# Two S4 convolution layers and SwiGLU layers on one core: a PSUM tile for each row tile of a down product, and the second chunk's exponents through TensorE

## The chip, the cores and the metric

One Trainium2 chip, one of its cores. The metric is the device time of one execution in microseconds; the time given for a kernel is the median of its runs. Engine names are those of the profile: PE is TensorE's matrix unit, PEld its weight loads, DVE is VectorE, ACT is ScalarE, POOL is GpSimd, SP is SyncE, whose queue issues most DMA transfers.

## What is computed

The input is one sequence of 2048 rows of 512 channels. It goes twice through a pair of layers, each added to its input after a layer norm:

```
K = real(sum_n C * exp(dt*A*l) * dt*B)          # [512, 2048], one kernel for both layers
y = causal convolution of layernorm(x) with K, over the 2048 rows, per channel
x = x + y + layernorm(x) * Dskip
h = layernorm(x);  x = x + (silu(h @ w_gate) * (h @ w_up)) @ w_down      # 512 -> 1376 -> 512
```

A has 128 complex states per channel. The convolution weights K are the same in both layers, so they are formed once.

## The kernel before, in words

**First stage, to about 300 us: the convolution weights.** The 512 channels are worked in 8 chunks of 64 (`ch`, lines 352 to 604). For a chunk, `re` and `im` hold the powers exp(dt*A*32a) for a = 0 to 64 with the 128 states on the partitions. They are made in parts:

- `gen_turns` and `gen_reduce` (DVE line 365, ACT lines 376 and 382, DVE lines 385 and 388) form the angles and take off whole turns; `gen_trig` (ACT lines 395 to 397) makes sines and cosines of them.
- The magnitudes exp(32a*rho) go to `re` (a = 1 to 32) and `mu` (a = 33 to 63). For chunks 2 to 7, `gen_mags` lets PE form the exponents 32a*rho as a matrix product into PSUM (line 438) and ACT takes one Exp over 1024 elements for each of four parts (line 441). The product's left side, `lts`, is rho split into three bf16 parts by POOL (`parts`, lines 423 to 426) and transposed by two DMAs (`turned`, line 430); its right side is a constant table (`tab`), loaded at line 989. For chunks 0 and 1, `gen_exp` makes them on ACT alone: 39 Exp of 64 elements (line 412) and four Square (line 415).
- `gen_e` (DVE lines 450 to 459) multiplies the magnitudes in; `gen_g` (DVE lines 467 to 499, with two accumulating DMAs from POOL's queue, lines 495 and 500) forms the coefficients `g`.
- `lags` (PE lines 510 and 511) multiplies both into `pk` in PSUM, ACT copies it to `ks` (line 516), `spread` (PE line 526) lays it out, ACT copies it to `kt`, and `spectra` (PE line 547) transforms it; ACT and DVE write the spectra out (lines 556 and 584 to 588).

Beside this, PE transforms the first two blocks of 512 normed rows by `direct` (line 286; the list `fw` for block 0, `early` and `second` for block 1). Block 0's rows are scaled by `norm_early` (DVE line 278). `gen_w` (DVE lines 183 to 187) forms the products dt*B*C for `g`. In this stage the order on PE, DVE and ACT is the order of the code, in which generators are advanced by hand (`take(g, 1)`); POOL and SP are ordered by a scheduler.

**Second stage.** The rows are worked in blocks of 512; `SEQ` gives the order of (layer, block). `ssm` of the next block (transform of its rows, DVE products with the spectra, lines 762 and 765, inverse transform on PE, line 781) is interleaved with `ffn` of the present one. `ffn` works two halves of 256 rows. For a half it makes six gate and up products `pgu` (PE lines 886 to 888; the remainder columns at lines 853 to 855), each evacuated by ACT (Silu, line 891; copy, line 893) and DVE (lines 892 and 894) into the fp16 pair `hh` and `hl`. Then comes the down product `py` (PE lines 900 to 902): 33 matmuls for each of its two row tiles of 128 rows. DVE scales each and adds it to `xt` (line 905), and a DMA stores the rows. In this stage a scheduler orders all engines; it tracks waits by tile.

`pgu`, `py`, and in the first stage `pm`, `pk` and `kp` come from one PSUM pool, `big`, of two slots, each of two banks:

```
    def pbig(shape, name):
        return ps.tile(shape, F32, name=name, tag="big", bufs=2)
```

Of the kernel before, what the change touches and what calls it, by code (L numbers as in the profile page):

```python
# [13 lines left out]
BF16 = mybir.dt.bfloat16  # L14
I32 = mybir.dt.int32
AF = mybir.ActivationFunctionType
OP = mybir.AluOpType
# [5 lines left out]
P = 128  # L23
# [58 lines left out]
def kernel(ctx, tc, x, a_re, a_im, b_re, b_im, c_re, c_im, log_dt, d_skip,  # L82
# [317 lines left out]
    def gen_exp(ch, ts):  # L400

        re, im, mu, xz, mz, t16 = ts
        r_ = rho[:, ch * DC:(ch + 1) * DC]
        for lv, m in enumerate(ZP):
            A.activation(mz[:, lv], r_, AF.Exp, scale=float(m))
            yield
        G.memset(re[:, :, 0], 1.0)
        if ch > 1:
            return
        for a0, o in ((0, re), (32, mu)):  # L410
            for a in [a for a in range(a0 + 1, a0 + 33) if a < 64 and (a % 2 or a % 8 == 0)]:
                A.activation(o[:, :, a - a0], r_, AF.Exp, scale=32.0 * a)
                yield
            for st in (2, 4):
                A.activation(o[:, :, st:33:2 * st] if a0 == 0 else o[:, :, st::2 * st],
                             re[:, :, (a0 + st) // 2:(a0 + 34) // 2:st], AF.Square)
                yield
# [11 lines left out]
        for c in range(2):  # L429
            nc.sync.dma_start_transpose(lts[:, c], pt[:, c].rearrange("p g q d -> p (g q d)"))  # L430

    def gen_mags(ch, ts):

        for k, o in enumerate((ts[0][:, :, 1:33], ts[2][:, :, 1:])):
            for h in range(2):
                pm = pbig([P, 32, 32], "pm")
                for e in range(2):
                    PE.matmul(pm[:, 16 * e:16 * e + 16], lhsT=lts[:112, ch % 2, h], rhs=tab[:112, k, e],
                              start=True, stop=True)
                yield  # L440
                A.activation(o[:, 32 * h:32 * h + 32], pm[:, :, :32 - k], AF.Exp)
                yield
# [426 lines left out]
    def ffn(layer, b, ready=None):  # L869
        for s in range(T // TB):  # L870
            rows = TB // P
            xt = xs[SEQ.index((layer, b)) % 3][:, s * rows:(s + 1) * rows]
            nh, nlo = ready if ready and s == 0 else ffn_norm(layer, b, s)
            hh = tl([P, FT, TB], "hh", "hh", F16)
            hl = tl([P, FT, TB], "hl", "hl", F16)
            for f0 in (0, 2, 4, 6, FT - 1, 8) if ready and s == 0 else (FT - 1, 0, 2, 4, 6, 8):
                pgu = pbig([P, 2, 2, TB], "pgu")
                if f0 == FT - 1:
                    remainder(pgu, nh, nlo, hh, hl)
                    continue  # L880
                for i in range(2):
                    fs = slice((f0 + i) * P, (f0 + i + 1) * P)
                    for wi in range(2):
                        o = pgu[:, wi, i]
                        for k in range(4):
                            PE.matmul(o, lhsT=wgu(wi, k, 0)[:, fs], rhs=nh[:, k], start=k == 0, stop=False)  # L886
                            PE.matmul(o, lhsT=wgu(wi, k, 0)[:, fs], rhs=nlo[:, k], start=False, stop=False)  # L887
                            PE.matmul(o, lhsT=wgu(wi, k, 1)[:, fs], rhs=nh[:, k], start=False, stop=k == 3)  # L888
                with tc.high_priority(offset=BOOST):
                    sg = tl([P, 2, TB], "sg", "sg")  # L890
                    A.activation(sg, pgu[:, 0], AF.Silu, scale=sc6[:, 3:4])  # L891
                    V.scalar_tensor_tensor(sg, pgu[:, 1], sc6[:, 4:5], sg, OP.mult, OP.mult)  # L892
                    A.activation(hh[:, f0:f0 + 2], sg, AF.Copy)  # L893
                    V.tensor_tensor(hl[:, f0:f0 + 2], sg, hh[:, f0:f0 + 2], OP.subtract)  # L894
            py = pbig([P, rows, D], "py")
            for r in range(rows):
                rc = slice(r * P, (r + 1) * P)
                for f in range(FT):
                    n = min(P, F - f * P)
                    PE.matmul(py[:, r], lhsT=hh[:n, f, rc], rhs=wd(f, 0)[:n], start=f == 0, stop=False)  # L900
                    PE.matmul(py[:, r], lhsT=hh[:n, f, rc], rhs=wd(f, 1)[:n], start=False, stop=False)  # L901
                    PE.matmul(py[:, r], lhsT=hl[:n, f, rc], rhs=wd(f, 0)[:n], start=False, stop=f == FT - 1)  # L902
                c = s * rows + r
                with tc.high_priority(offset=BOOST):
                    V.scalar_tensor_tensor(xt[:, r], py[:, r], sc6[:, 5:6], xt[:, r], OP.mult, OP.add)  # L905
                    if layer == NL - 1:
                        nc.sync.dma_start(out[0, b * T + c * P:b * T + (c + 1) * P, :], xt[:, r])
                    else:
                        nc.sync.dma_start(xdr[b, c], xt[:, r])
# [15 lines left out]
    with tc.manual_schedule(engines={mybir.EngineType.Activation, mybir.EngineType.DVE, mybir.EngineType.PE}):  # L925
# [10 lines left out]
        tr = gen_trig(ts[0])  # L936
        take(tr, 5)
        take(ex, 11)
        gen_w()
        norm_early(xe, ne, stats_x)  # L940
        fw = [direct(0, h, q, [ne[:, c, h * HD:(h + 1) * HD] for c in range(4)]) for h in range(2) for q in QORD]
        for f in fw:
            next(f)
# [8 lines left out]
        take(fw[1], 1)  # L952
        stats_x = stats(x1, 4, 1.0)
        take(fw[2], 1)
        for g in (gg, ge, gg, ge, gg, ge, gg, ge, gg, rd, gg, rd, gg, rd, gg, rd, gg, rd, rd, rd):
            take(g, 1)
        tr = gen_trig(ts[1])
        take(tr, 1)
# [12 lines left out]
        for g in (gg, ge, ge, gg, ge, ge):  # L971
            take(g, 1)
        ex = gen_exp(1, ts[1])
        take(ex, 14)
        take(fw[6], 1)
        take(ex, 13)
        take(fw[7], 1)
        mags = None
        take(early[0], 1)
        sp = iter(())  # L980
        for i in range(NCH - 1):
# [22 lines left out]
            norm_units(3, 9)  # L1004
            norm_units(0, 0)
            ks = spread_in(pk)
            if i == 0:
                take(early[1], 1)
            if mags:
                take(mags, 1)  # L1010
            if i % 2 == 0 and 0 < i < NCH - 2:
# [4 lines left out]
            if more:  # L1016
                rd = gen_reduce(ts[i + 2])
                next(rd)
            for g in (None, gg, None, gg, ge, gg, ge, gg, None, gg, None, rd, rd, ge, rd, rd, ge, rd, rd, rd, rd):
                take(g, 1) if g else wrap()  # L1020
            while tops:
# [19 lines left out]
            if more:  # L1041
                sp = spectra(i, kt, 0, NB, late=True)
                take(sp, 1)
                ex = gen_exp(i + 2, ts[i + 2])
                take(ex, 100)
                mags = gen_mags(i + 2, ts[i + 2])
                take(mags, 2)
                norm_units(3, 9)
                take(sp, 2)
                take(mags, 2)  # L1050
                take(sp, 2)
                norm_units(0, 0)
                sizes(i, kt, ks)
                take(ge, 2)
                wrap()
                take(ge, 1)
                wrap()
                take(ge, 1)
                take(gg, 1)
                while tops:  # L1060
                    tops.pop(0)()
                ts[i] = gs[i] = None
            else:
                sizes(i, kt, ks)
                take(ge, 4)
                take(gg, 1)
# [116 lines left out]
```

## Time and profile before

| | |
|---|---|
| runs shown | 1187.15, 1191.75 and 2940.31 us, median 1191.75 |
| the profiled execution | 1189.7 us, of which the traced span 1187.9 us |
| PE busy | 1108.9 us, 93% of the span |
| DVE busy | 1017.2 us, 86% |
| ACT busy | 621.3 us, 52% |
| POOL busy | 112.9 us, 10% |

A busy share is an average over stages. Matmuls overlap in the records, so the pace of PE is read from the distance between the starts of two matmuls, not from the length of one. An idle time in a list of waits stands with what ended it: "PE py L900 <- DVE xg L905" is time in which PE stood before a matmul of line 900 until the DVE instruction of line 905 was done. In a timeline the idle time before an instruction stands at the row's end, in brackets. "xne", "xg", "xf" and "mix" are the program's names for buffers that hold rows and their parts at that time.

### The profile page before, as it was taken

To read this page: it belongs to the slowest core of one execution; us is meant where nothing else is said; L and a number is where in the kernel's file an instruction comes from. 1 tells how busy PE (TensorE), PEld (TensorE's weight loads), DVE (VectorE), ACT (ScalarE), POOL (GpSimd) and SP (SyncE) were. 2 spreads that over 40 slices of the span, in tenths; PEclk is the share of its full clock that TensorE was granted. 3 is DMA by queue.
4 is the path that set the end of the run, shared out by engine and by line. 5 is a ranking of instruction groups with operands and counts; after the bars stand their busy time and mean duration, and the time that the engine had idled before them with its cause. 6 is when DMAs were issued, how large, how long until landed. Compare 5 with 4: busy or idle time off the path is not lost.

```text
span 1187.9 us, 25243 instructions
## 1 busy us (share of the span) xinstructions
PE 1108.9 (93%) x10268; PEld 862.1 (73%) x10268; DVE 1017.2 (86%) x1669; ACT 621.3 (52%) x1190; POOL 112.9 (10%) x166
## 2 busy tenths in 40 slices
PE   2999899889789989899999999999999999999998
PEld 2867677677675848687768687858687686877875
DVE  8979999998899998999999999989992899983211
ACT  6999889862383553538553534735432452334211
POOL 3100200004200010001000100111000010000000
PEclk9989999999899989999999999989999999999999
DMA  6445455577695238332343444324534144312000
GB/s 235 124 139 127 119 124 124 128 191 197 193 282 170 76 115 200 114 103 83 103 151 122 121 167 144 105 77 155 153 105 135 45 121 134 120 41 46 14 23 18
DMA packets 138455, 146.90 MB, mean 124 GB/s; under 512 B 77858, under 2 KB 87074, under 8 KB 138339
## 3 DMA queue, kind: packets, MB, share of 16 engines
q1 hardware_dynamic: 133474, 128.51, 36.0%
q0 software_dynamic: 4864, 16.78, 6.1%
q8 instruction: 80, 1.31, 0.5%
q14 instruction: 37, 0.30, 0.1%
HBM read 98.19 MB, written 28.31 MB: 106 GB/s over the span
## 4 chain that ended last, share of the span: by engine, by line
PE 37%; DVE 24%; issue 4%; ACT 3%; DMA 3%; SPq 1%; POOL 1%; DVEq 0%; ACTq 0%; POOLq 0%
PE pgu L886 5%; PE pgu L887 5%; PE pgu L888 5%; PE py L900 5%; PE py L901 5%; PE py L902 4%; DVE t L762 4%; PE pi L781 3%; DVE yk L765 3%; PE pf L270 3%; DVE z L226 2%; DVE yk L762 2%; DMA mix<-nn 2%; DVE sg L892 2%; DVE hl L894 2%
## 5 line engine op out<-in xcount | busy, mean ns | idle before, releaser
L886 PE MATMUL pgu<-mix,wsl 128*128 128x256 f16 x1280 | 351.1, 274 | 4.6 <-DVE mix L832 2.4
L887 PE MATMUL pgu<-mix,wsl 128*128 128x256 f16 x1280 | 351.1, 274 | 0.0
L888 PE MATMUL pgu<-mix,wsl 128*128 128x256 f16 x1280 | 350.9, 274 | 0.0
L900 PE MATMUL py<-wsl,hh 128*128 128x512 f16 (+1 forms) x352 | 135.4, 385 | 9.3 <-DVE xg L905 4.7
L887 PEld LDWEIGHTS <-wsl 128*128 128x128 f16 x1280 | 125.9, 98 | 22.2 <-issue 5.9
L886 PEld LDWEIGHTS <-wsl 128*128 128x128 f16 x1280 | 126.0, 98 | 16.6 <-issue 0.3
L902 PE MATMUL py<-wsl,hl 128*128 128x512 f16 (+1 forms) x352 | 135.3, 384 | 2.7 <-DVE hl L894 2.7
L888 PEld LDWEIGHTS <-wsl 128*128 128x128 f16 x1280 | 126.0, 98 | 15.4
L901 PE MATMUL py<-wsl,hh 128*128 128x512 f16 x320 | 123.3, 385 | 0.0
L762 DVE TENSOR_TENSOR t<-uu,w 128x1024 f32<-128x1024 f32 x96 | 116.7, 1216 | 0.2
L765 DVE TENSOR_TENSOR yk<-yk,t 128x1024 f32<-128x1024 f32 x96 | 116.6, 1215 | 0.1
L891 ACT ACTIVATE sg<-pgu,sc 128x512 f32<-128x512 f32 x80 | 54.4, 680 | 106.5 <-PE pgu L888 100.2
L892 DVE SCALAR_TENSOR_TENSOR sg<-pgu,sc,sg 128x512 f32<-128x512 f32 x80 | 59.5, 744 | 50.6 <-ACT sg L891 50.4
L781 PE MATMUL pi<-yl,mix 128*128 128x256 f16 x672 | 91.6, 273 | 8.6 <-ACT yl L770 6.8
L547 PE MATMUL pw<-kt,ek 128*128 128x256 f32 (+2 forms) x420 | 95.9, 365 | 0.0
L893 ACT ACTIVATE hh<-sg 128x512 f16<-128x512 f32 x80 | 50.0, 626 | 78.5 <-DVE sg L892 78.3
L547 PEld LDWEIGHTS pw<-kt,ek 128*128 128x128 f32 x420 | 76.3, 190 | 9.1
L270 PE MATMUL pf<-z,eh 128*128 128x256 f16 x576 | 76.0, 273 | 0.0
L770 ACT ACTIVATE yl<-mix,sy 128x512 f16<-128x512 f32 x56 | 40.2, 718 | 64.5 <-DVE mix L767 64.3
L781 PEld LDWEIGHTS <-mix 128*128 128x128 f16 x672 | 65.1, 98 | 12.1 <-issue 2.2
L762 DVE TENSOR_TENSOR yk<-u,w0r 128x1024 f32<-128x1024 f32 x56 | 68.0, 1215 | 0.9 <-ACT u L272 0.9
L901 PEld LDWEIGHTS <-hh 128*128 128x128 f16 (+1 forms) x352 | 34.8, 99 | 46.4 <-issue 11.8
(247 smaller groups left out, 2182.9 us busy)
## 6 DMA issues: line engine op xcount, KB each, us to landing
w<-wdr SPq DMA_DIRECT2D x96, 256.0 KB, 2.7
uu<-udr SPq DMA_DIRECT2D x96, 256.0 KB, 3.0
udr<-u POOLq DMA_DIRECT2D x32, 256.0 KB, 2.5
wdr<-wo SPq DMA_DIRECT2D x96, 64.0 KB, 2.7
udr<-u SPq DMA_DIRECT2D x16, 256.0 KB, 2.2
g<-tmp POOLq DMA_DIRECT2D x8, 512.0 KB, 4.5
g<-btl POOLq DMA_DIRECT2D x8, 512.0 KB, 5.9
n<-xdr SPq DMA_DIRECT2D x4, 1024.0 KB, 5.6
```

The source lines that it names most:

```text
L270: PE.matmul(pf[:, o], lhsT=e, rhs=m, start=k == 0, stop=k == len(terms) - 1)
L547: PE.matmul(pw[:, i], lhsT=e, rhs=kt[:, :, c + 4 * k0:4 * k1:4, :].rearrange("p g k d -> p k g d"), start=c == 0, stop=c == 3)
L762: V.tensor_tensor(t, uu.unsqueeze(1).to_broadcast([P, 2, 2, HD]), w.unsqueeze(2).to_broadcast([P, 2, 2, HD]), OP.mult)
L765: V.tensor_tensor(yk, yk, t, OP.add)
L781: PE.matmul(pi[:, o], lhsT=e, rhs=m, start=k == 0, stop=k == len(terms) - 1)
L886: PE.matmul(o, lhsT=wgu(wi, k, 0)[:, fs], rhs=nh[:, k], start=k == 0, stop=False)
L887: PE.matmul(o, lhsT=wgu(wi, k, 0)[:, fs], rhs=nlo[:, k], start=False, stop=False)
L888: PE.matmul(o, lhsT=wgu(wi, k, 1)[:, fs], rhs=nh[:, k], start=False, stop=k == 3)
L892: V.scalar_tensor_tensor(sg, pgu[:, 1], sc6[:, 4:5], sg, OP.mult, OP.mult)
L900: PE.matmul(py[:, r], lhsT=hh[:n, f, rc], rhs=wd(f, 0)[:n], start=f == 0, stop=False)
L901: PE.matmul(py[:, r], lhsT=hh[:n, f, rc], rhs=wd(f, 1)[:n], start=False, stop=False)
L902: PE.matmul(py[:, r], lhsT=hl[:n, f, rc], rhs=wd(f, 0)[:n], start=False, stop=f == FT - 1)
```

## The change

Three things change.

- In `ffn` each of the two row tiles of a down product gets a `big` tile of its own ([128, 512]) in place of one tile [128, 2, 512] for both.
- For chunk 1, `gen_exp` stops after the first six Exp (line 405), and `gen_mags` forms the magnitudes as for the later chunks. For it, `parts(0)` and `turned()` run early, and the table is loaded a first time into a tile `tab1` of the buffer `nn`, which `bw` held before.
- Orders: `norm_early` comes ahead of `gen_w` on DVE. In the list of steps before chunk 1's sines, the six steps of `rd` (turns taken off chunk 1) come early between those of `gg` and those of `ge` late. In the first round of the loop the second block's last evacuation (`take(early[1], 1)`) comes later.

```diff
@@ gen_exp @@
         G.memset(re[:, :, 0], 1.0)
-        if ch > 1:
+        if ch:
             return
@@ gen_mags @@
-    def gen_mags(ch, ts):
+    def gen_mags(ch, ts, tab):
@@ ffn @@
-            py = pbig([P, rows, D], "py")
             for r in range(rows):
+                py = pbig([P, D], "py")
                 rc = slice(r * P, (r + 1) * P)
                 for f in range(FT):
                     n = min(P, F - f * P)
-                    PE.matmul(py[:, r], lhsT=hh[:n, f, rc], rhs=wd(f, 0)[:n], start=f == 0, stop=False)
-                    PE.matmul(py[:, r], lhsT=hh[:n, f, rc], rhs=wd(f, 1)[:n], start=False, stop=False)
-                    PE.matmul(py[:, r], lhsT=hl[:n, f, rc], rhs=wd(f, 0)[:n], start=False, stop=f == FT - 1)
+                    PE.matmul(py, lhsT=hh[:n, f, rc], rhs=wd(f, 0)[:n], start=f == 0, stop=False)
+                    PE.matmul(py, lhsT=hh[:n, f, rc], rhs=wd(f, 1)[:n], start=False, stop=False)
+                    PE.matmul(py, lhsT=hl[:n, f, rc], rhs=wd(f, 0)[:n], start=False, stop=f == FT - 1)
                 c = s * rows + r
                 with tc.high_priority(offset=BOOST):
-                    V.scalar_tensor_tensor(xt[:, r], py[:, r], sc6[:, 5:6], xt[:, r], OP.mult, OP.add)
+                    V.scalar_tensor_tensor(xt[:, r], py, sc6[:, 5:6], xt[:, r], OP.mult, OP.add)
@@ the order of the first stage @@
         take(ex, 11)
+        norm_early(xe, ne, stats_x)
         gen_w()
-        norm_early(xe, ne, stats_x)
+        parts(0)
+        turned()
+        tab1 = tl([P, 4 * HD], "tab1", "nn")
+        nc.sync.dma_start(tab1, c_am[:, NA:])
...
-        for g in (gg, ge, gg, ge, gg, ge, gg, ge, gg, rd, gg, rd, gg, rd, gg, rd, gg, rd, rd, rd):
+        for g in (gg, ge, gg, rd, gg, rd, rd, gg, rd, rd, gg, rd, gg, rd, gg, rd, gg, ge, gg, ge, ge):
             take(g, 1)
...
         ex = gen_exp(1, ts[1])
-        take(ex, 14)
+        mags = gen_mags(1, ts[1], tab1.bitcast(BF16).rearrange("p (k e d a) -> p k e d a", k=2, e=2, d=16))
+        take(ex, 100)
+        take(mags, 2)
         take(fw[6], 1)
-        take(ex, 13)
+        take(mags, 5)
         take(fw[7], 1)
-        mags = None
...
-            if i == 0:
-                take(early[1], 1)
             if mags:
                 take(mags, 1)
...
+            if i == 0:
+                take(early[1], 1)
             for g in (None, gg, None, gg, ge, gg, ge, gg, None, gg, None, rd, rd, ge, rd, rd, ge, rd, rd, rd, rd):
...
-                mags = gen_mags(i + 2, ts[i + 2])
+                mags = gen_mags(i + 2, ts[i + 2], tab)
```

**PE at the border between the two row tiles of a down product**, in the last half of the last block. Before: the last matmul of row tile 0, then the first of row tile 1. Both write the same tile, py_13499; hh and hl are the activations' two parts, wsl2 and wsl3 hold the weights.

```order
L902 MATMUL py_13499<-wsl3_3119,hl_13169 128x512
L900 LDWEIGHTS hh_13168
L900 MATMUL py_13499<-wsl2_3118,hh_13168 128x512 [waits DVE_49]
L901 LDWEIGHTS hh_13168
L901 MATMUL py_13499<-wsl2_3118,hh_13168 128x512
```

Now, the same half: row tile 0 is py_13495 and row tile 1 is py_13531.

```order
L902 MATMUL py_13495<-wsl3_3100,hl_13165 128x512
L900 LDWEIGHTS hh_13164
L900 MATMUL py_13531<-wsl2_3099,hh_13164 128x512 [waits DVE_49]
L901 LDWEIGHTS hh_13164
L901 MATMUL py_13531<-wsl2_3099,hh_13164 128x512
...
L900 LDWEIGHTS hh_13164 [waits Activation_49]
L900 MATMUL py_13495<-wsl3_3100,hh_13164 128x512
```

Row tile 1 is begun while row tile 0 is still open; the wait on DVE that its first matmul keeps is the one for a free slot (the last `pgu` read by DVE), and matmuls of row tile 1 stand ahead of row tile 0's that need the last `hh` and `hl`. Before, it waited for line 905 of row tile 0.

**ACT where chunk 1's magnitudes are made**, the difference, with the evacuations (L289) and the copies behind.

```order
 L405 ACTIVATE mzp<-rho 128x64 x6
-L412 ACTIVATE re<-rho 128x64 x8
-L289 ACTIVATE u<-pf 128x512
-L412 ACTIVATE re<-rho 128x64 x12
-L415 ACTIVATE re<-re 128x64x8
+L441 ACTIVATE re<-pm 128x32x32
+L289 ACTIVATE u<-pf 128x512
+L441 ACTIVATE re<-pm 128x32x32
+L441 ACTIVATE mu<-pm 128x32x31
 L289 ACTIVATE u<-pf 128x512 x2
-L415 ACTIVATE re<-re 128x64x4
-L412 ACTIVATE mu<-rho 128x64 x19
```

43 instructions became four, which wait for PE's products `pm`.

**DVE behind the start of `g` for chunk 0.** Before:

```order
L479 TENSOR_TENSOR btl<-g,xi 128x2x192
L450 TENSOR_TENSOR im<-im,re 128x4x8x32
L481 TENSOR_TENSOR g<-g,btl 128x192
L482 TENSOR_TENSOR g<-g,btl 128x192
L453 TENSOR_TENSOR re<-re 128x4x8x32
L486 TENSOR_TENSOR g<-g,xr 128x2x256
```

Now:

```order
L479 TENSOR_TENSOR btl<-g,xi 128x2x192
L385 TENSOR_TENSOR xi<-xi,xr 128x384
L481 TENSOR_TENSOR g<-g,btl 128x192
L482 TENSOR_TENSOR g<-g,btl 128x192
L388 SCALAR_TENSOR_TENSOR im<-t_171,re 128x64x16
L388 SCALAR_TENSOR_TENSOR im<-t_171,re 128x64x8
```

The steps that take turns off chunk 1 (L385, L388), which read what ACT wrote at lines 376 and 382, stand where chunk 0's magnitudes were multiplied in (L450, L453); these come later.

## The prediction

> **What bounds the kernel now.** I read the table of stages first (each row: a stretch in us, its length, then busy us of PE, PEld, DVE, ACT and POOL with instruction counts, then the granted clock).
>
> ```profile
> 60.00:90.00 30.00, 27.14 (x245) 19.80 (x236) 23.34 (x33) 29.89 (x68) 2.07 (x4) 0.89 0.51 137
> 120.00:150.00 30.00, 26.76 (x386) 21.05 (x385) 29.95 (x46) 25.60 (x46) 8.53 (x8) 1.00 0.50 120
> 510.00:540.00 30.00, 30.00 (x278) 26.89 (x276) 29.68 (x55) 13.85 (x25) 2.17 (x4) 1.00 0.39 124
> 900.00:930.00 30.00, 28.85 (x255) 24.63 (x253) 9.40 (x19) 14.09 (x32) 1.35 (x1) 1.00 0.24 84
> 1110.00:1140.00 30.00, 30.00 (x252) 21.72 (x250) 7.30 (x11) 6.05 (x10) 0.20 (x1) 1.00 0.03 10
> ```
>
> From 60 to 90 us ACT never rests and DVE has 6.7 us of idle time: chunk 1's magnitudes and chunk 2's angles pass through ACT there. From then on DVE is full in the first stage (29.95 of 30). In the second stage PE and DVE are both full, but at 900 us DVE has little to do while PE works on, and in the end PE works alone. So PE holds the backlog of the second stage: idle time of PE taken away before that point comes out of the end, as long as DVE has its 20 us of slack at 900.
>
> Next the list of waits from 330 us on, PE's first, then what DVE waits for at line 905.
>
> ```profile
> PE pi L781 <- ACT yl L770: 6.8, 5, 1.9
> PE py L900 <- DVE xg L905: 4.7, 4, 2.5
> PE py L900 <- DVE xf L905: 3.7, 3, 1.6
> PE py L902 <- DVE hl L894: 2.7, 2, 2.0
> DVE xg L905 <- PE py L902: 39.4, 9, 7.6
> ```
>
> The largest group on PE, 4.7 + 3.7 = 8.4 us in 7 waits, is a down product that waits for its own half's line 905: row tile 1 goes to another half of the tile than the one line 905 reads, but the tile is one. The 39.4 us on DVE fall mostly after 900 us, where DVE has nothing else; they are no gain to be had.
>
> **The change part by part: the down products.** The waits of PE, in the timeline (start, length, instruction, and in brackets the idle time before it):
>
> ```profile
> 435.02 0.22 PE L853 MATMUL pgu<-wsl,mix 128*128 128x96 f16 x1 [2.01 <-DMA mix<-nn]
> 436.29 0.58 PE L900 MATMUL py<-wsl,hh 128*128 128x512 f16 x1 [1.01 <-DVE xg L905]
> 436.67 0.63 PE L901 MATMUL py<-wsl,hh 128*128 128x512 f16 x1
> ...
> 501.98 0.38 PE L900 MATMUL py<-wsl,hh 128*128 128x512 f16 x1 [2.54 <-DVE xg L905]
> 502.19 0.38 PE L901 MATMUL py<-wsl,hh 128*128 128x512 f16 x1
> ```
> ```profile
> 436.00:442.00 6.00, 5.71 (x14) 2.02 (x14) 5.99 (x11) 3.26 (x7) 0.00 (x0) 0.50 0.61 181
> ```
>
> A wait costs itself, and once more when the clock falls behind it: from 436.67 on the starts lie 0.43 us apart (6 us hold 14 of them), at 502 0.21, and the granted clock of 436 to 442 is 0.50. Those 14 matmuls cost 14 x 0.215 = 3.0 us on top. With a tile for each row tile the 8.4 us go. Of the 3.0 us I take half, 1.5, since two idle times precede the dip and only one of them is removed. The Trainium skill (TensorE: Matmul & The Clock Gate, Part 1) has the clock fall after an idle window of about 3.4 us and come back after as long a busy one; by that rule the 2.01 and the 1.01 us were needed together, all 3.0 us would go, and the sum below would be 1.5 us lower. The trace agrees as far as it goes: after the lone 2.54 us at 501.98 the clock stayed up.
>
> Row tile 1 now also stands ahead of the matmuls that wait for the last hh and hl, so the 2.7 us before line 902 should shrink; I take 1.5 of them. Together 8.4 + 1.5 + 1.5 = 11.4 us.
>
> What this adds: both slots of the pool are held by down products at a half's end. The next half's remainder (lines 853 to 855), which filled the border before, has to wait for line 905 of row tile 0. Behind that wait stand all of PE's products of the next half and ssm's transforms. The cover is row tile 1, 33 matmuls at 0.215 us, 7.1 us, against the 2.5 us that was the longest wait for line 905; so I cost the wait itself at nothing, and at 2.5 us for some halves if the cover is gone. The orders of all engines in this stage are also drawn anew, and what filled a hole may no longer stand there. No row prices that; bounds are nothing and the whole 11.4 (each hole reopens elsewhere). I take 3.4, near the lower end, because the waits of PE by other causes are single ones of 2 us and less. Second stage: 11.4 - 3.4 = 8 us less; bounds 0 and 14.
>
> **Chunk 1's magnitudes and the orders around them.** Rows of ACT around it (the last two are where ACT comes to chunk 0's ks and chunk 2's xr), and what the work costs by form:
>
> ```profile
> 50.98 1.12 ACT L395 ACTIVATE re<-im 128x1024 f32<-128x1024 f32 x1 [1.06 <-DVE im L388]
> 68.79 1.02 ACT L516 ACTIVATE ks<-pk 128x1024 f32<-128x1024 f32 x1
> 70.17 0.53 ACT L376 ACTIVATE xr<-xi 128x384 int32<-128x384 f32 x1
> ```
> ```profile
> L412 ACT ACTIVATE re<-rho 128x64 f32<-128x64 f32 x20 | 3.3, 315 | 0.0
> L412 ACT ACTIVATE mu<-rho 128x64 f32<-128x64 f32 x19 | 2.9, 303 | 0.0
> L415 ACT ACTIVATE mu<-re 128x512 f32<-128x512 f32 x1 | 1.1, 1146 | 0.0
> L415 ACT ACTIVATE re<-re 128x512 f32<-128x512 f32 x1 | 1.1, 1117 | 0.0
> L415 ACT ACTIVATE re<-re 128x256 f32<-128x256 f32 x1 | 0.7, 695 | 0.0
> L415 ACT ACTIVATE mu<-re 128x256 f32<-128x256 f32 x1 | 0.7, 693 | 0.0
> ```
> ```profile
> L441 ACT ACTIVATE re<-pm x12: 1017/1026/1045, 86.3 to 244.1; 128x1024 f32<-128x1024 f32 x12
> L438 PE MATMUL pm<-kt,btl x48: 377/379/390, 82.7 to 252.5; 112*128 112x512 bf16 x48
> ```
>
> Removed: 3.3 + 2.9 + 3.6 = 9.8 us of ACT. Added: four Exp, 4.1 us of ACT, and eight matmuls of PE, 8 x 0.38 = 3 us at most. PE has room: with norm_early ahead of gen_w its first transforms begin earlier.
>
> ```profile
> 18.04 1.21 DVE L183 TENSOR_TENSOR bw<-bw,dt 128x1024 f32<-128x1024 f32 x1
> 22.89 2.13 DVE L278 TENSOR_SCALAR xne<-xne,rs 128x512 f32<-128x512 f32 x4
> 33.61 1.21 DVE L450 TENSOR_TENSOR im<-im,re 128x1024 f32<-128x1024 f32 x1
> 35.22 0.52 ACT L376 ACTIVATE xr<-xi 128x384 int32<-128x384 f32 x1
> 52.99 2.29 DVE L459 TENSOR_TENSOR re<-re,mu 128x992 f32<-128x992 f32 x2
> 57.15 0.56 DVE L467 TENSOR_TENSOR xr<-xr,mzp 128x384 f32<-128x384 f32 x1 [1.87 <-ACT mzp L405]
> 57.61 0.37 PE L510 MATMUL pk<-re,g 128*32 128x64 f32 x8
> 62.78 0.33 PE L511 MATMUL pk<-im,g 128*32 128x64 f32 x4
> 63.14 1.23 DVE L450 TENSOR_TENSOR im<-im,re 128x1024 f32<-128x1024 f32 x1 [1.37 <-ACT re L415]
> 70.73 0.56 DVE L385 TENSOR_TENSOR xi<-xi,xr 128x384 f32<-128x384 f32 x1 [2.69 <-ACT xr L376]
> 89.42 0.36 DVE L584 TENSOR_TENSOR wo<-s 128x192 f32<-128x192 f32 x1 [2.04 <-ACT s L556]
> ```
>
> The swap is worth 22.89 - 18.04 = 4.9 us to PE's first matmul alone; it then waits for ACT's evacuations, and ACT is busy there. It moves nothing on DVE.
>
> DVE's idle times before 90 us are 1.87 + 1.37 + 2.69 + 2.04 = 8.0 us: the most that this part can give. Step by step:
>
> - New on DVE: line 385 for chunk 1 now comes where the second L450 stood, at 33.6 us. It needs ACT's xr, done at 35.22 + 0.52 = 35.74. A stall of 2.1 us, and all of DVE behind it. The end of gen_e, after the two L459, moves from 55.3 to 57.4.
> - ACT itself no longer has the 1.06 us before 50.98, since DVE's line 388 for chunk 1 is now done early; its Exp of line 405 end at 56.0 and not at the 57.1 at which L467 could start. So DVE's 1.87 us are gone, but against the stall: L467 starts at 57.4, 0.3 late. The 1.37 us before L450 go too.
> - ACT then does the four Exp with one evacuation between. The third must be done before pk may have its slot: 56.0 + 1.0 + 0.5 + 1.0 + 1.0 = 59.5. What is late next is therefore lags: pk starts 1.9 us later than at 57.61 and, as long as before (63.1 - 57.6 = 5.5 us), ends at 65.0. ACT copies it by 66.0 and comes to xr at once: 4.1 us before the 70.17.
> - DVE reaches line 385 for chunk 2 at about 66.9, and xr is there at 66.5: no wait, 3.8 us earlier than 70.73. PE's pk, one transform of 3.5 us and the spread then end about 1 us later than ACT would like (an estimate from their 1.9 us delay against ACT's lead), which leaves ACT, and DVE's L584, 3 us earlier than 89.42.
>
> From there DVE is full, so 3 us stay; bounds 0 (lags' delay reaches DVE in full) and 8.0.
>
> At nothing I cost: POOL's four steps for parts(0), since POOL is busy for 2 of 30 us at 60; the table's further load, 512 KB like the one in the row below, issued when gen_w is done and needed only for the four Exp at 56 us; the transpose for the next pair of chunks, which on SP now waits for chunk 1's last product, with two stores of block 1's spectra inputs and the loads for `second` behind it, needed only after the spread. If that cover is gone, PE's transform there comes late by some us and the 3 us are lost.
>
> ```profile
> kt<-in_c_am_dram SPq DMA_DIRECT2D x1, 512.0 KB, 5.4
> ```
>
> **The sum.** Span 1187.9 - 8 - 3 = 1176.9; around it lie 1189.7 - 1187.9 = 1.8 us, so 1178.7 against the profiled 1189.7. The runs shown have the median 1191.75, 2.1 above the profiled one, and their lowest is 2.6 below it; I say 1179, 1.1% under the median.
>
> **The rivals.**
>
> - *The waits are only moved.* DVE is full from 366 to 870 us, so PE, freed of line 905, waits for `yl` instead (the 6.8 us above grow). For it: 29.68 of 30 us on DVE at 510. Against it: DVE's idle 20 us at 900. Then only the first stage pays: 1189.7 - 3 = 1187.
> - *Both slots held: slower.* The next half's remainder waits for line 905 of row tile 0, queued on DVE behind ssm's products. It decides from the point where DVE needs more than the 7.1 us of row tile 1 to come to line 905. Each of the 16 halves would pay some 1.2 us (8.4 / 7): 1189.7 + 19 - 3 = 1206. Against it: the longest wait for line 905 was 2.5 us. If moreover the clock dips once in each half (3.0 us as at 436), it is 16 x 3.0 = 48 more, 1254, slower by over 2%. The same page of the Trainium skill names such a case (A second HAM failure mode): products of 512 columns cycling through PSUM banks with short idle times between, and a clock that swings. In this trace one dip stands behind two waits, and none behind the lone 2.54 us, so I give it little.
> - *More than the sum.* All of DVE's 8.0 us in the first stage and the whole 14 us (8.4 + 3.0 + 2.7) in the second: 1189.7 - 22 = 1168; with a hole or two of other cause closed by the new order, below.
>
> **How the numbers follow.** The forecast 0.60; moved waits 0.22; both slots held 0.05, with dips 0.03 more; more than the sum 0.10. The range takes in the forecast's bounds and the moved waits: from 1167, a microsecond under the largest sum, to 1192, moved waits with the first stage's gain lost as well. A measurement of this kernel tells about 2% from no change, that is 24 us: faster by over 2% (under 1168) 0.10, within 2% 0.87, slower by over 2% 0.03.
>
> **What would show it.** Right: no wait of line 900 for line 905 in the list; PE's idle time from 366 us on smaller by some 8 us; DVE without the waits at 57 and 70 us, with one of about 2 us near 34; line 584's first instruction near 86.4. Wrong: waits of lines 853 or 886 for line 905, a clock under 1.00 at the halves' borders, waits of `pi` that grow by what those of `py` lose, or DVE at 89 us where it was.

## The result and the profile after

The changed kernel takes 1174.31 us (median of 6 runs, 1173.08 to 1175.68); the kernel before, run beside it, 1189.37 (median of 6 runs: five of 1185.36 to 1191.75 and the one of 2940.31). The ratio is 0.9875, its 95% interval 0.9849 to 0.9901: faster by 1.25%. In a second measurement (after_again, below) the ratio was 0.9878 (0.9849 to 0.9908). The profiled execution's span is 1173.0 us against 1187.9, so 14.9 us are to be found in the trace.

**They split at line 832.** This is DVE's instruction that ends the first stage's tail, 323.52 us after the start in the kernel before; here, in the timeline of the kernel after:

```profile
319.23 1.23 DVE L832 TENSOR_TENSOR mix<-pt,mix 128x1024 f16<-128x1024 f32 x1 [3.77 <-ACT mix L830]
```

So in these two profiles 4.3 us came in the first stage and 10.6 in what follows. Line 832 comes at 319.2 to 319.4 us in four of the five profiles of kernels with the new first stage and at 324.7 in the fifth (shared_late, below); the two with the old one have 323.3 and 323.5.

**First stage.** The timeline of the kernel after, DVE's rows at the places that the prediction worked through, then ACT's from chunk 1's exponents to chunk 2's `xr`:

```profile
35.76 0.56 DVE L385 TENSOR_TENSOR xi<-xi,xr 128x384 f32<-128x384 f32 x1 [1.75 <-ACT xr L376]
57.46 0.55 DVE L467 TENSOR_TENSOR xr<-xr,mzp 128x384 f32<-128x384 f32 x1
67.31 0.55 DVE L385 TENSOR_TENSOR xi<-xi,xr 128x384 f32<-128x384 f32 x1
85.86 0.36 DVE L584 TENSOR_TENSOR wo<-s 128x192 f32<-128x192 f32 x1 [2.36 <-ACT s L556]
```
```profile
55.25 1.02 ACT L441 ACTIVATE re<-pm 128x1024 f32<-128x1024 f32 x1
56.17 0.58 ACT L289 ACTIVATE u<-pf 128x512 f32<-128x512 f32 x1
56.64 1.03 ACT L441 ACTIVATE re<-pm 128x1024 f32<-128x1024 f32 x1
57.64 1.00 ACT L441 ACTIVATE mu<-pm 128x992 f32<-128x992 f32 x1
...
59.49 1.03 ACT L441 ACTIVATE mu<-pm 128x992 f32<-128x992 f32 x1
...
65.19 1.02 ACT L516 ACTIVATE ks<-pk 128x1024 f32<-128x1024 f32 x1 [3.14 <-PE pk L511]
66.11 0.52 ACT L376 ACTIVATE xr<-xi 128x384 int32<-128x384 f32 x1
```

DVE has the new stall of 1.75 us, and no wait before lines 467 and 385 at 57 and 67 us. ACT goes through the four Exp without idle time, so neither table, transposes nor products are late for them. The last of them ends 0.5 us past 60; `xr` for chunk 2 comes at 66.11, 4.1 us earlier than before, and line 584 at 85.86, 3.6 us earlier.

**Second stage.** PE's waits from 330 us on (total us, how many, the longest), three smaller ones of before that the prediction did not show, then the kernel after:

```profile
PE pgu L853 <- DVE sg L892: 2.3, 1, 2.3
...
PE pgu L886 <- DVE xg L905: 0.7, 1, 0.7
PE pgu L886 <- DVE sg L892: 0.7, 2, 0.4
```

```profile
PE pi L781 <- ACT yl L770: 5.5, 3, 2.2
PE pgu L853 <- DVE sg L892: 3.4, 1, 3.4
PE pgu L855 <- DMA mix<-nn: 2.5, 1, 2.5
PE pgu L886 <- DVE sg L892: 2.4, 4, 1.1
PE pgu L886 <- DVE xg L905: 2.3, 2, 1.7
PE pf L270 <- DVE z L226: 1.7, 2, 1.1
PE pgu L886 <- DVE xf L905: 1.5, 1, 1.5
```

Line 900 no longer waits for line 905, nor 902 for `hl`: 11.1 us of waits are gone. But others came: the next half's products (886) wait 3.8 us for line 905, where it was 0.7, and the remainder (853) and 886 wait 5.8 us for the `sg` of line 892, where it was 3.0. Beside these, 855 waits 2.5 us for a DMA, and `pf` 2.2 us. All waits of PE after line 832 add up to 29.3 us before and 24.5 after. That is 4.8 of the 10.6 us.

**Most of the rest is the clock.** The table of windows (columns as in the prediction; the third number from the end is the granted clock), first the kernel before at its two dips behind 400 us, then the kernel after at its only one there:

```profile
434.00:438.00 4.00, 1.97 (x7) 0.75 (x8) 4.00 (x9) 2.13 (x3) 0.00 (x0) 0.68 0.78 220
438.00:442.00 4.00, 4.00 (x11) 1.43 (x10) 3.99 (x8) 2.15 (x5) 0.00 (x0) 0.50 0.41 105
442.00:446.00 4.00, 4.00 (x19) 1.77 (x18) 2.48 (x4) 1.83 (x5) 0.72 (x1) 0.96 0.35 126
783.00:784.00 1.00, 1.00 (x5) 0.45 (x4) 1.00 (x2) 0.72 (x1) 0.00 (x0) 0.82 0.00 0
784.00:788.00 4.00, 3.37 (x15) 1.98 (x14) 4.00 (x10) 1.89 (x4) 0.00 (x0) 0.50 0.42 131
788.00:792.00 4.00, 4.00 (x28) 3.04 (x27) 3.18 (x8) 0.37 (x1) 0.00 (x0) 0.69 0.17 66
```
```profile
444.00:448.00 4.00, 4.00 (x32) 3.07 (x29) 4.00 (x9) 2.79 (x9) 0.71 (x1) 0.57 1.00 358
```

One minus the clock, times the length, is the time that a dip costs a busy PE. Before, the rows from 434 to 446 give (0.32 + 0.50 + 0.04) x 4 = 3.4 us, those from 783 to 792 0.18 + (0.50 + 0.31) x 4 = 3.4 us. After, one is left, 0.43 x 4 = 1.7 us. (Every kernel has dips between line 832 and 370 us as well; they are in the sums below.) The waits around them, first in the timeline of before, then in that of after; the prediction shows those at 435 and 436 us:

```profile
782.58 0.39 PE L902 MATMUL py<-wsl,hl 128*128 128x512 f16 x1 [2.04 <-DVE hl L894]
...
785.38 0.37 PE L886 MATMUL pgu<-mix,wsl 128*128 128x256 f16 x1 [0.63 <-DVE sgr L862]
```
```profile
435.50 0.27 PE L781 MATMUL pi<-yl,mix 128*128 128x256 f16 x1 [1.74 <-ACT yl L770]
439.31 0.22 PE L853 MATMUL pgu<-wsl,mix 128*128 128x96 f16 x1 [1.21 <-DMA mix<-nn]
443.41 0.22 PE L855 MATMUL pgu<-wsl,mix 128*128 128x96 f16 x1 [2.53 <-DMA mix<-nn]
```

Of the two waits at each dip of the kernel before, only the first stands ahead of it. The clock falls at about 783.6, 1.1 us after the wait of 2.04 us and before that of 0.63; and at 435.5, while the second wait is still going on, which ends at 436.29:

```profile
435.50:436.50 1.00, 0.21 (x1) 0.10 (x1) 1.00 (x4) 0.89 (x2) 0.00 (x0) 0.50 0.99 264
```

The dip after is behind the same products as the one at 436, those of the remainder that wait for `mix` from a DMA. split_only (below) has the second stage's same order there, and the same waits within 0.1 us (1.73, 1.13 and 2.49 us), and its clock stays at 1.00.

With this the second stage can be accounted for. I summed, over windows of 1 us from line 832 to PE's last matmul, PE's idle time, and one minus the clock times PE's busy time; idle time at a low clock is thus counted once, as idle. What remains of the stretch to the end should be PE's work and the 4 to 5 us behind its last matmul, the same in every kernel (the others are those of the experiments below):

| kernel | line 832 to the end | PE idle | clock lost while busy | remains |
|---|---|---|---|---|
| before | 864.4 | 28.3 | 11.9 | 824.2 |
| first_only | 860.7 | 26.5 | 10.3 | 823.9 |
| shared_late | 859.6 | 26.9 | 7.7 | 825.0 |
| split_only | 851.9 | 22.6 | 5.8 | 823.5 |
| after | 853.8 | 23.6 | 6.9 | 823.3 |
| after_again | 853.9 | 24.4 | 6.1 | 823.4 |
| both_chunks_2 | 850.5 | 21.4 | 6.1 | 823.0 |
| small_slots | 912.2 | 65.5 | 22.1 | 824.6 |

It does remain, within 2.0 us, so PE bounds this stage, and a kernel's time there is its work, its waits and its dips. From before to after: 4.7 us of idle time, 5.0 of clock, 0.9 of the remainder.

That nearly half is clock is one profile against one, and the runs do not settle how much of it lasts. They have only the mean granted clock of a whole execution: 0.9834 in the 52 runs of the kernel before whose clock is on record, 0.9877 in 12 of the changed one. One minus the clock, times each run's time, averages 19.7 and 14.5 us; the mean times are 13.5 us apart. Of these 5.2 us a part falls in the first stage, where the clock loss differs from profile to profile (8.8 us before, 7.5 in after, 2.7 in after_again) and need not cost time: chunk 0's products into `pk` took 6.4 us in small_slots, at a clock of 0.50 for 5.1 of them, and 6.4 us in both_chunks, at 1.00. split_only, whose first stage is that of before, averages 16.9 us over 12 runs, 2.8 less than the kernel before; first_only, which leaves the second stage as it was, 16.8.

### The profile page after: what moved, and what is told of

The parts are those of the page before. It is cut to its first block, busy times and chain, and to the rows that moved or that the text cites. A ratio compares the mean times of both kernels' runs of the same rounds, so it can differ in the third digit from the quotient of the medians.

```text
span 1173.0 us, 25233 instructions
## 1 busy us (share of the span) xinstructions
PE 1103.5 (94%) x10276; PEld 861.6 (73%) x10276; DVE 1019.0 (87%) x1669; ACT 617.2 (53%) x1151; POOL 117.0 (10%) x170
## 4 chain that ended last, share of the span: by engine, by line
PE 40%; DVE 30%; ACT 13%; issue 9%; DMA 5%; POOL 2%; SPq 1%; DVEq 0%; ACTq 0%; POOLq 0%
PE pgu L886 6%; PE pgu L887 6%; PE pgu L888 6%; DVE yk L765 4%; DVE t L762 4%; PE pi L781 4%; PE pw L547 4%; PE py L900 3%; PE py L901 3%; PE py L902 3%; DVE z L226 2%; DVE yk L762 2%; PE pf L270 2%; DVE bt L226 2%; PE pk L510 2%
## 5 line engine op out<-in xcount | busy, mean ns | idle before, releaser
L886 PEld LDWEIGHTS <-wsl 128*128 128x128 f16 x1280 | 125.8, 98 | 14.9
L902 PE MATMUL py<-wsl,hl 128*128 128x512 f16 (+1 forms) x352 | 132.8, 381 | 0.0
L894 DVE TENSOR_TENSOR hl<-sg,hh 128x512 f16<-128x512 f32 x80 | 55.2, 691 | 13.5 <-ACT hh L893 13.5
```

The lines of the kernel that those rows point to most:

```text
L902: PE.matmul(py, lhsT=hl[:n, f, rc], rhs=wd(f, 0)[:n], start=False, stop=f == FT - 1)
```

## The experiments

**split_only and first_only: each part alone.** The first is the kernel before with only this, the second the changed kernel with only this undone:

```diff
-            py = pbig([P, rows, D], "py")
             for r in range(rows):
+                py = pbig([P, D], "py")
... (py for py[:, r] in the lines behind)
```

> The kernel before with only the second-stage change: a PSUM tile for each row tile of a down product; the first stage is the one of before. Theory A, the two parts are separate and the second stage gains what PE no longer waits for at the border of the row tiles (first lines 905 seen 5.3 us later relative to before, last 14.7 us earlier, so about 10 to 11 us): 1178 to 1180 us against 1189. Theory B, the gain in the second stage hangs on the first stage's earlier end or on a lucky new order: less than 6 us, 1184 or more. In the list of waits from 330 us on, line 900 waits for line 905 no more under both.

> The kernel before with only the first-stage changes (chunk 1's exponents through PE, norm_early ahead of gen_w, the new order of the steps, the later second evacuation of early); the down product has one tile for both row tiles, as before. Theory A: line 584 starts near 85.9 as in the changed kernel and the 3.6 to 4.3 us stay to the end: about 1185 us against 1189. Theory B, the first stage brings most: 1180 or less. Waits of line 900 for line 905 stay some 8 us.

split_only: 1177.06 us against 1185.86, ratio 0.9927 (0.9901 to 0.9953). first_only: 1181.85, ratio 0.9954 (0.9927 to 0.998). The product is 0.9881, the whole change 0.9875: within the intervals the parts add, and neither needs the other. With the mean of before, 1187.6 us, they are 8.7 and 5.5 us, each with an interval of 3 us to either side; by split_only's own theories that is nearer to A (10 to 11 us) than to B (under 6). PE's waits in split_only, then in first_only:

```profile
PE pgu L886 <- DVE xg L905: 2.7, 2, 1.7
PE pgu L853 <- DVE sg L892: 2.7, 1, 2.7
PE pgu L886 <- DVE xf L905: 1.5, 1, 1.5
```
```profile
PE py L900 <- DVE xg L905: 4.7, 4, 2.5
PE py L900 <- DVE xf L905: 3.8, 3, 1.6
PE py L902 <- DVE hl L894: 2.0, 1, 2.0
```

The waits of each are those of the kernel whose `ffn` it has.

**shared_late: the waits of line 900 removed, but one tile kept.** The additions go into a loop of their own behind both row tiles' matmuls, so row tile 1 no longer has to wait for them:

```diff
+            py = pbig([P, rows, D], "py")
             for r in range(rows):
-                py = pbig([P, D], "py")
...
+            for r in range(rows):
                 c = s * rows + r
... (py[:, r] for py in the lines between and behind)
```

> The changed kernel, but with one PSUM tile for both row tiles as before, and both instructions of line 905 placed behind the second row tile's matmuls, so that no matmul of row tile 1 can wait for line 905 of row tile 0 and only one slot of the pool is held. Theory A1, the removed wait is what paid: within 3 us of the changed kernel, 1172 to 1178. Theory A2, the slot of its own is what paid (row tile 0 is added and stored early, the next half's products find a free slot): 1180 to 1186, most of the second stage's gain gone.

1181.33 us, ratio 0.9955 (0.9927 to 0.9983), the same as first_only, as theory A2 has it. Its waits:

```profile
PE pgu L886 <- DVE xg L906: 6.2, 4, 3.8
PE pgu L886 <- DVE xf L906: 3.9, 2, 2.2
```

The 8.4 us of waits before line 900 have become 10.1 us before line 886 (line 906 here is the addition): the slot comes free only when both row tiles have been added, and the next half's products wait for it. So to take the wait away is not enough; what pays is that row tile 0 is added, and its slot comes free, while row tile 1 is still being multiplied. (Which of the two counts, the free slot or the early addition itself, this run does not separate; its waits are for the slot.) In its profile the clock lost is 4.2 us less than in the kernel before (table above), but over its 12 runs the mean clock was 0.9845 against 0.9834, 1.4 us of the whole execution, so little of that lasts. The profiled run's first stage ended late, at 324.70 us, after a wait of DVE for `xr` of 3.2 us that the kernel after does not have there; so its time is read from the 12 runs.

**small_slots: the down product in the smaller pool.** If the two big slots are what is short, row tiles of 512 columns could go to the pool of one-bank slots, in which the transforms write `pf` and `pi`:

```diff
-                py = pbig([P, D], "py")
+                py = psml([P, D], "py")
```

> The changed kernel with the down products' tiles taken from the other PSUM pool tag, of four slots of one bank each, which the ssm's transforms use too; the two large slots then serve the gate and up products alone. If the held slots cost something in the changed kernel (line 886 waits 2.3 + 1.5 us for line 905, 853 waits for 892 3.4 us): 2 to 5 us faster, 1169 to 1172. If not, or if the ssm's products now wait for small slots: the same or up to 8 us slower.

1231.58 us, ratio 1.0376 (1.0335 to 1.0417): slower by far more than expected. Waits and windows of this kernel:

```profile
PE pi L781 <- ACT yl L770: 40.7, 11, 7.7
PE pf L270 <- ACT z L260: 7.5, 1, 7.5
```
```profile
386.00:390.00 4.00, 0.98 (x5) 0.62 (x5) 3.23 (x4) 1.15 (x4) 3.35 (x1) 0.84 0.41 133
390.00:394.00 4.00, 1.79 (x9) 1.09 (x8) 3.86 (x8) 3.66 (x6) 0.11 (x1) 0.50 0.01 3
394.00:398.00 4.00, 0.00 (x0) 0.00 (x0) 4.00 (x12) 0.22 (x2) 0.00 (x0) 0.50 0.37 131
```

No product waits for line 905 any more, and PE stands 48.2 us behind `yl` and `z` instead, where the kernel after has 5.5 and 0.5. That shows the place: ssm's chain of evacuations is late for PE. Why it is late is open: that `py` holds small slots which ssm's `pf` and `pi` need, or that the scheduler drew another order, was not told apart. The clock goes down with it: 22.1 us of PE's busy time are lost from line 832 on, where the kernel after has 6.9. Idle time and clock together explain this kernel too (table above).

**no_swap, no_order, no_mags: the parts of the first stage, each undone in the changed kernel.**

```diff
@@ no_swap @@
-        norm_early(xe, ne, stats_x)
         gen_w()
+        norm_early(xe, ne, stats_x)
@@ no_order @@
-        for g in (gg, ge, gg, rd, gg, rd, rd, gg, rd, rd, gg, rd, gg, rd, gg, rd, gg, ge, gg, ge, ge):
+        for g in (gg, ge, gg, ge, gg, ge, gg, ge, gg, rd, gg, rd, gg, rd, gg, rd, gg, rd, rd, rd):
@@ no_mags: chunk 1's exponents on ACT again, no table and parts ahead @@
-        if ch:
+        if ch > 1:
             return
...
```

> The changed kernel with gen_w ahead of norm_early again, as before the change. One look; what is read is the start of the first line 584 on DVE (89.42 us before, 85.86 in the changed kernel) and PE's first line 286. Theory: the swap brings PE's first transform forward by 4.9 us and nothing on DVE, since PE then waits for ACT's evacuations: line 584 at 85.9 within 0.3. Rival: PE's earlier end carries into lags, and without the swap line 584 comes 1 to 2 us later, since chunk 1's products then stand behind transforms that end 4 us later.

> The changed kernel with the steps before chunk 1's sines in the order of before (ge early, rd late), chunk 1's exponents still through PE. One look. Theory: DVE's stall of 1.75 us at 35.8 us goes, but ACT waits for lines 385 and 388 again (0.4 and 1.1 us), so line 467 waits for line 405 as before, and line 584 comes 0.5 to 1.5 us later than in the changed kernel, near 87. Rival: the order costs as much as it brings, line 584 at 85.9 or earlier.

> The changed kernel with chunk 1's exponents on ACT again (39 Exp of 64 elements and four Square), with no early table, split or transposes; the other orders stay changed. One look. Theory: this is where the first stage's gain comes from, line 584 near 89 or later (ACT comes to chunk 0's ks some 4 us later). Rival: the orders alone bring half of it, line 584 at 87.5 or earlier.

One run each, so the times (1172.56, 1179.02 and 1174.71 us) tell little; the trace tells more, if a common start is used. The early loads end up to 1.4 us apart from run to run. So I count from DVE's instruction that forms `rho` (line 930) to the first of line 584:

| kernel | `rho` | line 584 | distance |
|---|---|---|---|
| before | 9.89 | 89.42 | 79.5 |
| split_only | 9.52 | 89.03 | 79.5 |
| after, after_again, first_only, shared_late | 9.87 to 10.91 | 85.26 to 87.12 | 75.4 to 76.2 |
| no_swap | 10.70 | 87.58 | 76.9 |
| no_order | 10.25 | 88.13 | 77.9 |
| no_mags | 9.55 | 87.42 | 77.9 |
| both_chunks | 10.21 | 85.88 | 75.7 |
| both_chunks_2 | 10.13 | 85.06 | 74.9 |

The four kernels with the full first stage spread over 0.9 us (a fifth, small_slots, has 76.0). Undone singly, the steps cost about 1 us (swap), 2 (order, a little more than expected) and 2 (exponents) of the 3.3 to 4.2. The exponents bring no more than the order of the steps: without them the kernel still keeps about half of the gain, as the rival said, and the theory that the gain is theirs falls. The swap's 1 us is on the edge of the spread, but the trace shows a cause for it, the one the rival named: without the swap PE's first transform starts at 24.30 us and not at 18.61, chunk 1's products start at 57.01 and not at 53.02 (0.8 us of each difference is the later start), and ACT, which goes through the four Exp without idle time in the kernel after, waits for the first:

```profile
57.65 1.04 ACT L441 ACTIVATE re<-pm 128x1024 f32<-128x1024 f32 x1 [1.50 <-PE pm L438]
```

In no_order the old wait is back:

```profile
57.84 0.56 DVE L467 TENSOR_TENSOR xr<-xr,mzp 128x384 f32<-128x384 f32 x1 [1.86 <-ACT mzp L405]
```

**both_chunks and both_chunks_2: the idea carried on.** DVE's new stall at 35.76 comes from ACT, which makes chunk 0's magnitudes with 39 Exp and four Square; 31 of the Exp and the Squares stand right ahead of the evacuation of line 289. Here chunk 0 goes through PE too:

```diff
-        if ch:
-            return
+        return
...
+        tab0 = ts[0][2].rearrange("p d a -> p (d a)")[:, :4 * HD]
+        nc.sync.dma_start(tab0, c_am[:, NA:])
...
+        mags = gen_mags(0, ts[0], tab0.bitcast(BF16).rearrange("p (k e d a) -> p k e d a", k=2, e=2, d=16))
-        for f in fw:
+        for f, n in zip(fw, (1, 1, 1, 1)):
+            next(f)
+            take(mags, n)
+        for f in fw[4:]:
             next(f)
```

> The changed kernel with chunk 0's exponents through PE as well: its table is loaded early into the space of mu, PE makes the four products between the first transforms, and ACT takes four Exp in place of 39 Exp and four Square. ACT, which is busy from 10 to 57 us, loses some 5 us before its first evacuation at 34.7 us. Theory, ACT sets the pace there: the evacuation starts near 31, DVE's stall of 1.75 us goes, line 584 comes at 82.5 to 84, and the time is 2 to 3 us under the changed kernel. Rival, DVE is the bound (its work up to line 459 of chunk 0 is the same, and it has only that stall to lose): line 584 at 84 or later, time the same within 2 us.

1175.38 us, ratio 0.988 (0.9847 to 0.9914): nothing gained. ACT's timeline shows why:

```profile
27.36 1.97 ACT L444 ACTIVATE re<-pm 128x1024 f32<-128x1024 f32 x2
32.97 1.89 ACT L444 ACTIVATE mu<-pm 128x992 f32<-128x992 f32 x2 [3.64 <-PE pm L442]
34.74 0.60 ACT L289 ACTIVATE u<-pf 128x512 f32<-128x512 f32 x1
```

ACT needs four Exp where it had 35 instructions from 27 us on, but waits 3.64 us ahead of the third, until PE has done the fourth product at 32.9 us, which stands behind further transforms. Line 289, and with it `xr`, comes at 34.74 as in the kernel after. This profile's first stage then ended late, at 326.17 us, after single waits of DVE at 157 and 166 us (2.6 us for a DMA and 3.3 for `xr`, the latter as in shared_late); so here too the time is read from the runs. both_chunks_2 puts products three and four directly behind the second transform, `(1, 2, 1, 0)`, and ran beside the changed kernel:

> Both chunks through PE as in both_chunks, but the third and fourth product stand right behind the second transform of block 0, so that ACT's four Exp can follow one another. Theory (ACT's idle 1.89 us and the late first evacuation of both_chunks came from the place of the two products on PE): first evacuation L289 near 32 us in place of 34.7, DVE's stall of 1.75 us at L385 gone, L584 first at 84 to 85 us in place of 85.9, time 1 to 2 us under the changed kernel, which runs beside it (ratio to the kernel before 0.985 to 0.987). Rival (ACT's pace before 35 us does not set what follows, DVE is bound by its own work up to pk): the stall goes but L584 starts within 0.5 us of 85.9 and the time is as in the changed kernel.

> The changed kernel once more, on the chip on which both_chunks_2 runs, so that the two are compared on one chip: ratio to the kernel before 0.9875 within the interval seen (0.985 to 0.990), L584 first at 85.9 us. If both_chunks_2 is the better one by its theory, its ratio is lower by 0.001 to 0.002; by the rival the two agree.

(The 1.89 us in the first of these texts is the length of two Exp; the idle time is the 3.64.)

```profile
27.30 1.96 ACT L444 ACTIVATE re<-pm 128x1024 f32<-128x1024 f32 x2
29.94 1.89 ACT L444 ACTIVATE mu<-pm 128x992 f32<-128x992 f32 x2 [0.68 <-PE pm L442]
31.71 0.60 ACT L289 ACTIVATE u<-pf 128x512 f32<-128x512 f32 x1
```

The idle time is down to 0.68 us, line 289 comes 3.0 us earlier, DVE's stall at line 385 is gone, and line 584 starts at 85.06. The time is 1172.45 us, ratio 0.9863 (0.983 to 0.9896); after_again has 1174.96 and 0.9878. The theory is right on the cause of the idle time; on the time nothing is shown, since the intervals overlap in the main. It is the kernel with the lowest median, and not shown to be faster than the change. Nor is its lead from the first stage. DVE's line 832 (848 there) starts at 320.09, not earlier than in after; its lead of 0.8 us at line 584 is lost again in DVE's waits for ACT's `s` (6.7 us between 84 and 300 us, 5.9 in after) and for `pi` (7.3 against 6.2). Its span is 2.4 us shorter than that of after, and the 3.3 us that make it so lie behind line 832, in waits and clock (the table above).

after_again also shows how much one profile of one kernel differs from the next. A wait of PE and the clock behind it:

```profile
498.31 0.37 PE L886 MATMUL pgu<-mix,wsl 128*128 128x256 f16 x1 [2.54 <-DVE xg L905]
```
```profile
498.00:502.00 4.00, 3.69 (x20) 2.64 (x20) 4.00 (x9) 0.72 (x1) 0.00 (x0) 0.57 0.21 74
```

In the first profile of the same kernel the wait at this place was 0.60 us and had no dip, but one stood at 444.

## Why the prediction was right, and where it was not

The forecast was 1179 us; it came to 1174.3, inside the range and its likeliest case: a gain from both parts, the larger from the second stage.

- *First stage, 3 us predicted.* 3.6 at line 584, 4.3 at line 832 in the profiles, 5.5 (2.4 to 8.7) by the runs of first_only. The chain that the prediction worked out stands in the trace row by row: the stall near 34 us (2.1 predicted, 1.75 seen), line 467 at 57.4 (57.46), the last `pk` at 65.0 (65.15), `xr` 4.1 us earlier (4.1), line 584 at 86.4 (85.86). "What is late next is lags" was the step that made the difference between the 8.0 us of idle time and the 3 forecast, and it held: ACT now waits 3.14 us for `pk`. Two sizes in it were off and cancelled: `pk` started at 58.73 and not at 59.5, because ACT's Exp of line 405 ended at 55.3 and not at 56.0, and took 6.4 us and not 5.5. What I costed at nothing (the table, `parts`, the transposes) cost nothing that a row shows. One thing was wrong: that the swap "moves nothing on DVE". Without it ACT waits 1.50 us for `pm`, and line 584 comes about 1 us later.
- *Second stage, the 8.4 us before line 900.* They went, and the wait of line 902 went whole (2.7, of which I had taken 1.5).
- *"3.4 us for holes that reopen."* Mis-sized. 11.1 us of waits went and the sum fell by 4.8, so 6.3 reopened. 3.1 of them stand where the prediction had looked (886 for line 905), and "the wait itself at nothing" was wrong for three halves: line 886 waits for line 905 for 1.7, 1.5 and 0.6 us. 2.8 stand at 853 and 886 for `sg`, which it had not named. The waits for line 905 are the rival with both slots held, on a small scale: about 3 us in place of its 19.
- *"1.5 us of the dip."* Mis-sized the other way, and its reason fails. The prediction halved the dip because two idle times precede it. By the rows of the clock only one does: the clock was at 0.50 before the wait that the change removes had ended. So this trace gave no ground for counting half of it as gone. It also priced one dip, at 436 us; the trace of before has a second of equal size at 784 to 790, behind the 2.04 us wait of line 902, the longest in a group that the prediction quotes. In the profile after, the second is gone and the first is half as large; by the two profiles the clock gave 5.0 us where the forecast had 1.5, and how much of it lasts is open (above).
- *What starts a dip.* The Trainium skill's rule (TensorE: Matmul & The Clock Gate, Part 1) would, as the prediction worked it out, have the 436 dip go whole. In split_only and after_again it did, in after half of it stayed. Its size agrees: each dip behind 400 us in before, after and after_again costs 1.7 or 3.4 us, one or two stretches of 3.4 us at clock 0.50. Where it differs is what starts one: the Trainium skill asks for an idle window of about 3.4 us, and here a single wait of 2.04 us was enough at 782 us in the kernel before, one of 2.54 us at 498 us in after_again.

So the errors nearly cancelled: waits 6.5 predicted (9.9 less 3.4) and 4.7 to 4.8 found, clock 1.5 predicted and 5.0 found in the profiles; by the runs of split_only the second stage gave 8.7 us (5.6 to 11.8) where the forecast had 8. The mechanism was right in its main step, the removed waits; that the sum was near was partly luck.

- *The rivals.* Waits only moved: no, those of `pi` for `yl` fell from 6.8 to 5.5 us. shared_late is a kernel in which they do move, to line 886, and it lost the second stage's gain in its time. DVE had the slack on which the argument against it rested, and PE's gain shortened it: DVE's waits for the down product, 39.4 us before, are now, in the list of DVE's waits of the kernel after:

```profile
DVE xg L905 <- PE py L902: 32.1, 8, 5.7
```

What stays open: why one wait of 2.5 us is followed by a dip and another is not (501.98 in the kernel before had none, 498.31 in after_again has one; 443.41 in after has one, its like in split_only none), how much of the clock's gain lasts from run to run, and what makes `yl` late in small_slots.

## What to carry to other kernels

When a pool of two PSUM slots feeds a pipeline, ask when each slot comes free, not only who waits: moving the reader behind the matmuls removed the visible wait and brought it back at the next owner of the slot, while a tile for each row tile let half of the product's space go early. When PE bounds a stage, count its time as work plus idle time plus the clock lost while it is busy, over the whole stage, before and after; the three explain each kernel of the table to about 2 us, and the list of waits alone explains less than half of this stage's gain in the two profiles. Before the clock's part is called a gain, ask whether it is there in many runs. Undo the parts of a change one by one in the part where they look like one idea: here the reordering of DVE's steps was worth as much as the work taken off ACT, about 2 us each by one profile.

## What was not expected of the hardware

- A short wait can cost twice. In the kernel before, one of 2.04 us was followed by 6.9 us at half clock (3.4 us lost), and behind another, of 2.01 us, the clock fell within 0.5 us and stayed low as long. Waits of 2.5 us were followed by 3.4 us at half clock in two profiles and by none in two others. In small_slots, whose waits of up to 7.7 us are many, the clock lost while PE is busy grew from 6.9 to 22.1 us.
- At half clock not everything takes longer: chunk 0's products into `pk` (128x64, f32) took 6.4 us in small_slots, nearly all at a clock of 0.50, and in both_chunks at 1.00.
- The dips are not at the same place in two runs of one kernel (444 us in after, 498 in after_again, 1.7 us lost each), and single runs range widely: a mean clock of 0.975 to 0.991 in the kernel before, 0.985 to 0.992 in the changed one. Only the means over many runs, 19.7 and 14.5 us lost in the whole execution, tell them apart.
